# A fused top-k attention and gated feed-forward kernel: the start-up slots rearranged (whole-row scores, paired weight shifts, other chunk counts, two feed-forward items in slot 6)

## The chip, the cores and the metric

The kernel runs on one core of one Trainium2 chip. A core has five engines that work side by side, each through its own list of instructions in order: TensorE (PE, matrix products), VectorE (DVE), ScalarE (ACT), GpSimd (POOL) and SyncE (SP, which here only starts transfers). They wait for each other through semaphores. The metric is the time of one execution on the device in microseconds (us); three runs of the kernel before took 1415.8, 1416.53 and 1416.7 us, median 1416.53 us.

## The reference

Two blocks follow each other. The first is attention of 8 batches, 8 heads, 576 positions and 64 channels a head that keeps only the 32 largest scores of each row. The second multiplies every token by a first weight matrix, applies h·cos(h), and multiplies by a second one.

```python
scores = scale * np.matmul(q, k.transpose(0, 1, 3, 2))
kth = np.partition(scores, -top_k, axis=-1)[..., -top_k:-top_k + 1]
scores = np.where(scores >= kth, scores, -1000000000.0)
scores = scores - np.max(scores, axis=-1, keepdims=True)
attn = np.exp(scores)
attn = attn / (np.sum(attn, axis=-1, keepdims=True) + 1e-09)
attn_out = np.matmul(attn, v)                 # top_k = 32
x = attn_out.transpose(0, 2, 1, 3).reshape(4608, 512)
h = x @ w_in                                  # 512 x 2048
out = (h * np.cos(h)) @ w_out                 # 2048 x 512
```

All of it is computed to float32 accuracy; the two weight matrices arrive as 64-bit floats.

## The kernel before, in words

**Units and slots.** The 4608 tokens are cut into 36 blocks of 128 rows. A unit is one block of rows for one pair of heads, so there are 144 units, four to a block (`NP = 4`). The main loop calls `slot` once for each unit i from 0 to 143; the order in which `slot` issues instructions is the order on every engine. In slot i the DVE selects the top 32 of unit i, ACT and DVE finish the softmax of unit i-1 (`w`), and the probabilities of unit i-2 (`x`) are turned for the product with v. For the first slots they are turned by PE and ACT (`turn`), from slot 6 on by a copy on POOL (L411), a write to memory and a transposing transfer on SP's queue (`send`).

**The way of one unit.** `scores` makes the products of q and k on PE. A row of 576 scores does not fit one accumulator bank, so 448 columns go to a tile `sc` and the last 128 to a shared tile `rim`. Before the change the 128 rows of a unit are always computed as two halves of 64 rows (`halves_of`), since a block can straddle two batches; with two heads this is four products for `sc` and four for `rim`, each on a 64x64 quarter of the PE array. `take_scores` copies them to memory on ACT: L247 for the 448 columns, and L251 twice for the ends, once for each half of the rows, as the two halves put the heads into the banks in opposite order (`rim_bank`). Scores are computed one or two slots ahead, for two units in the even slots from slot 2 on.

The DVE then folds each row (columns j and j+288): L259 writes the larger of each two into `rest`, and POOL makes the smaller ones, `low`, by an integer sum (L275) and difference (L284). In slots 8 to 10 (`BUSY`) the DVE makes `low` itself (L267). `topk_round` runs four rounds of MAX8 (L351) and MATCH_REPLACE8 (L356) on `rest` and two on `low`. The first instruction of the next slot on the DVE is the reduction at L339, so the distance of two L339 is the length of a slot.

**Values and the feed-forward block.** In slots 5, 10, 14, 18 and so on, `values` multiplies the turned probabilities of the last four units by v (L473), and `take_values` scales the result into `xT` on the DVE (L489, L497). `take_values` stands in the last round of `topk_round`, before the last MAX8 pair on `low`. From `xT` the feed-forward block is fed in items: an `ff1` item is eight 128x128 products into half an accumulator bank (L551), an `ff2` item two products 128x512 (L626). The table `plan` says for each slot modulo 4 which kinds are tried at three places of the slot (`feed`); kind 0 is `ff1`, kind 1 is `ff2`. When a bank is full, `take_banks` copies it on ACT (L565, L567), then POOL reduces the argument (L587, L596), ACT takes the sine (L606, after loading its table, and L388 loads the table of the exponential again), and POOL multiplies (L613).

**Weights.** The two matrices come in 32 chunks of 128x512 (16 of `w_in`, 16 of `w_out`), loaded by `load_weights` (n chunks a slot) and decoded in three steps: ACT makes two float pieces (L133, L136, `decode_first`, near the end of a slot), the DVE shifts one of them left by three bits (L144, `decode_second`, one instruction a chunk, 128x512), and POOL adds the pieces (L154, `decode_third`). In slot 0 the last two steps stand at the end of the slot; in every later slot they stand between the third and the fourth round of the top-k. A `w_in` tile holds four chunks; `w_out` was 16 tiles.

Of the kernel before, what the change touches and what calls it, by code (L numbers as in the profile page):

```python
# [17 lines left out]
P = 128  # L18
# [12 lines left out]
def kernel(  # L31
# [52 lines left out]
    for i in range(DF // CW):  # L84
        w = consts.tile([P, NC, CW], F32, tag=f"w_in{i}", name=f"w_in{i}")
        w_in.append(w)
        for c in range(NC):
            cols = slice(words * i * CW, words * (i + 1) * CW)
            chunks.append((moe_w_in[c * P : (c + 1) * P, cols], w[:, c]))
    for f in range(NF):  # L90
        w = consts.tile([P, DM], F32, tag=f"w_out{f}", name=f"w_out{f}")
        w_out.append(w)
        chunks.append((moe_w_out[f * P : (f + 1) * P, :], w))
    CHUNKS, XB = 6, 3
# [8 lines left out]
    def load_weights(n, queue):  # L103
        for _ in range(n):
            i = wq["next"]
            if i >= len(chunks):
                return
            src, dst = chunks[i]
            if not DECODE:
                queue.dma_start(out=dst, in_=src)  # L110
                wq["next"] = wq["done"] = i + 1
                continue
            spare = i < 2 * NC + 10 and i % 2 == 1 and staged(1) < XB
            if spare:
                st = ffw.tile([P, CW, 2], I32, tag="x", name="st", bufs=XB)
            elif staged() + ff["live"] >= CHUNKS:
                return
            else:
                st = ffw.tile([P, CW, 2], I32, tag="g", name="st", bufs=CHUNKS)
            queue.dma_start(out=st.rearrange("p w i -> p (w i)"), in_=src)  # L120
            wq["loaded"].append((st, dst, int(spare)))
            wq["next"] = i + 1
# [4 lines left out]
    def decode_first(n):  # L127


        for _ in range(min(n, len(wq["loaded"]))):  # L130
            st, w, spare = wq["loaded"].popleft()
            lo, hi = st[:, :, 0], st[:, :, 1]
            nc.scalar.activation(  # L133
                out=w, in_=hi.bitcast(F32), func=AF.Prelu, scale=2.0**-111, alpha=2.0**32
            )
            nc.scalar.mul(out=lo, in_=lo.bitcast(U32), mul=2.0**-29)  # L136
            wq["second"].append((st, w, spare))

    def decode_second(n):

        for _ in range(min(n, len(wq["second"]))):
            st, w, spare = wq["second"].popleft()
            wi = w.bitcast(I32)
            nc.vector.tensor_scalar(  # L144
                out=wi, in0=wi, scalar1=3, scalar2=None, op0=ALU.logical_shift_left
            )
            wq["third"].append((st, w, spare))

    def decode_third():

        while wq["third"]:
            st, w, _ = wq["third"].pop()
            wi = w.bitcast(I32)
            nc.gpsimd.tensor_tensor(out=wi, in0=wi, in1=st[:, :, 0], op=ALU.add)  # L154
            wq["done"] += 1
# [6 lines left out]
    for t0 in range(0, B * S, P):  # L162
        parts, halves_of = [], []
        for i, a in enumerate((t0, t0 + TAIL)):
            b, q0 = a // S, a % S
            halves_of.append((b, q0, i * TAIL))
            if parts and parts[-1][0] == b:
                parts[-1][2] = P
            else:
                parts.append([b, q0, TAIL, i * TAIL])  # L170
        for hp in range(NP):
            units.append({"hp": hp, "tok": t0, "parts": parts, "halves_of": halves_of})
    NU = len(units)
# [56 lines left out]
    def scores(u):  # L230
        sc = u["sc"] = ps.tile([P, 2, 512], F32, tag="sc", name="sc", bufs=2)
        for to, k0, k1 in ((sc, 0, SB), (sc_ends[u["n"] % 2], SB, S)):
            for b, q0, r0 in u["halves_of"]:
                for j in range(2):
                    d = slice(j * D, (j + 1) * D)
                    st = pairs[b, u["hp"]]
                    nc.tensor.matmul(  # L237
                        to[r0 : r0 + TAIL, rim_bank(r0, j) if k0 else place(u["hp"], j), 0 : k1 - k0],
                        st["q"][d, q0 : q0 + TAIL],
                        st["k"][d, k0:k1],  # L240
# [4 lines left out]
    def take_scores(u):  # L245
        s = u["s"] = work.tile([P, 2, S], F32, tag="s", name="s", bufs=4)
        nc.scalar.copy(out=s[:, :, 0:SB], in_=u["sc"][:, :, 0:SB])  # L247
        ends = sc_ends[u["n"] % 2]
        for r0 in (0, TAIL):
            r, back = slice(r0, r0 + TAIL), rim_bank(r0, place(u["hp"], 0))  # L250
            nc.scalar.copy(out=s[r, :, SB:S], in_=ends[r, :: 1 - 2 * back])  # L251
# [64 lines left out]
    def topk_round(u, rnd, between=(), ahead=None):  # L316
# [11 lines left out]
        for k in range(TOPK // 16):  # L328
            more = k < TOPK // 16 - 1
            if ahead and not more:  # L330
                take_values(ahead)
            search(top[:, :, 1 + 8 * k : 9 + 8 * k, 1], low, low, more, () if more else between)
# [124 lines left out]
    def values(us):  # L457


        begun = set()  # L460
        for b, _, rows, r0 in us[0]["parts"]:
            r = slice(r0, r0 + rows)
# [188 lines left out]
    def can_second():  # L651
        if not second:
            return False
# [91 lines left out]
    def slot(i, u, w, x, z):  # L745
        n = (3, 4, 4, 4, 4, 3)[i] if i < NP + 2 else 2
        if i < NP:
# [10 lines left out]
        topk_round(u, 2)  # L758
        if i > 0:
            decode_second(NP)  # L760
# [4 lines left out]
        if z:  # L765
            take_banks()
        feed(*plan[i % NP][0])

# [15 lines left out]
        if i + 1 < NU:  # L784
            take_scores(units[i + 1])
        topk_round(u, 3, both(w), z)
        if i == 0:
# [103 lines left out]
```

## Time and profile before

The profiled execution took 1416.63 us; the profiler's span, from the first to the last instruction, is 1414.8 us, so 1.8 us lie outside it.

| | PE | DVE | ACT | POOL |
|---|---|---|---|---|
| busy us in the span | 1354.5 | 1346.2 | 1143.5 | 1164.6 |
| share of the span | 96% | 95% | 81% | 82% |

The DVE's slots, from the starts of its L339 instructions:

| slot | 1 | 2 | 3 | 4 | 5 | 6 | 7 | 8 | 9 | 10 | 11 | 12 | 13 |
|---|---|---|---|---|---|---|---|---|---|---|---|---|---|
| starts at us | 17.37 | 28.29 | 38.63 | 48.96 | 59.29 | 71.59 | 81.59 | 91.38 | 101.98 | 112.31 | 124.51 | 134.13 | 143.43 |
| length us | 10.92 | 10.33 | 10.34 | 10.33 | 12.30 | 10.00 | 9.79 | 10.59 | 10.33 | 12.20 | 9.62 | 9.29 | 8.99 |

From slot 13 on, three slots of four take 8.99 us and the fourth, which has the `xT` instructions, mostly 9.6 to 9.9 us. The last unit's slot starts at 1347.47 us; what follows is the rest of the feed-forward block.

How to read it: a busy share says how much of a stretch an engine had an instruction in work, not that it set the pace. The pace is seen where an engine stands idle and from what released it. PE's busy time is partly modelled and holds waiting that it cannot show; the granted clock of PE (the share of full speed) is printed beside it by stretches.

### The profile page before, as it was taken

The numbers are of one execution on the slowest core, as the hardware profiler recorded it, in microseconds if no ns is written. First come the engines' busy times: TensorE is split into PE (matmuls) and PEld (weight loads), VectorE is DVE, ScalarE is ACT, GpSimd is POOL, SyncE is SP. The second block draws the span as 40 slices with busy tenths as digits, with TensorE's granted clock in tenths as the row PEclk, the third lists the DMA queues.
The fourth block names the chain that finished last, engine by engine and source line by source line (L and its number), as shares of the span: only waits on it lengthen the run. The fifth ranks groups of instructions, "written<-read, shape, count | busy, mean of one in ns | idle before, by whom it ended". The sixth has DMA issues, their size and how long they took to land.

```text
span 1414.8 us, 32526 instructions
## 1 busy us (share of the span) xinstructions
PE 1354.5 (96%) x11328; PEld 975.1 (69%) x11328; DVE 1346.2 (95%) x5161; ACT 1143.5 (81%) x2050; POOL 1164.6 (82%) x804
## 2 busy tenths in 40 slices
PE   4567999999999999999999999999999999999998
PEld 2355777777777777777777777777777777777775
DVE  7999999999999999999999999999999999999931
ACT  7978888888888888888888888888888888888831
POOL 4778889888988888888888888888888898888810
PEclk6688999999999999999999999999999999999999
DMA  9575776566765566657665666656766566665540
GB/s 284 174 231 157 208 214 173 159 172 189 170 178 157 166 173 185 176 150 206 172 170 154 157 180 183 183 149 188 191 168 169 150 174 169 144 157 145 152 100 16
DMA packets 427445, 240.15 MB, mean 170 GB/s; under 512 B 375952, under 2 KB 392592, under 8 KB 427280
## 3 DMA queue, kind: packets, MB, share of 16 engines
q1 hardware_dynamic: 420720, 224.22, 58.2%
q10 hardware_dynamic: 6560, 13.85, 2.7%
q8 instruction: 89, 1.46, 0.4%
q14 instruction: 76, 0.62, 0.1%
HBM read 45.09 MB, written 101.19 MB: 103 GB/s over the span
## 4 chain that ended last, share of the span: by engine, by line
PE 82%; DVE 9%; ACT 6%; DMA 1%; POOL 1%; issue 0%; SPq 0%; ACTq 0%; DVEq 0%; POOLq 0%
PE o L626 32%; PE mm L551 32%; PE rim L473 10%; PE sc L237 7%; DVE top L351 4%; DVE rest L356 2%; PE rim L237 2%; DMA st<-in_moe_w_in_dram 1%; ACT s L388 1%; ACT s L380 1%; DVE rest L259 1%; ACT st L136 1%; DVE low L356 1%; ACT w_in L133 0%; ACT w_out L133 0%
## 5 line engine op out<-in xcount | busy, mean ns | idle before, releaser
L551 PEld LDWEIGHTS mm<-xT,w_in 128*128 128x128 f32 x4608 | 538.3, 192 | 78.7 <-issue 56.0
L551 PE MATMUL mm<-xT,w_in 128*128 128x128 f32 x4608 | 540.3, 276 | 10.1 <-ACT x L567 8.4
L626 PE MATMUL o<-w_out,g 128*128 128x512 f32 x1152 | 524.7, 599 | 0.0
L351 DVE MAX8 top<-rest 128x8 f32<-128x288 f32 x1152 | 479.0, 451 | 0.0
L356 DVE MATCH_REPLACE8 rest<-top,rest 128x288 f32<-128x288 f32 x864 | 376.7, 444 | 0.0
L626 PEld LDWEIGHTS o<-w_out,g 128*128 128x128 f32 x1152 | 207.7, 190 | 219.5 <-issue 219.2
L411 POOL COPY halves<-s 128x2304 uint16<-128x2304 uint16 x140 | 294.5, 2103 | 51.7 <-ACT s L388 48.4
L351 DVE MAX8 top<-low 128x8 f32<-128x288 f32 x576 | 241.9, 449 | 0.5 <-POOL low L284 0.5
L388 ACT ACTIVATE s<-s,nd 128x576 f32<-128x576 f32 x288 | 220.3, 768 | 0.8
L284 POOL TENSOR_TENSOR low<-low,rest 128x576 int32<-128x576 int32 x141 | 199.2, 1413 | 11.1
L380 ACT ACTIVATE s<-s,top 128x576 f32<-128x576 f32 x288 | 205.5, 761 | 0.0
L275 POOL TENSOR_TENSOR low<-s 128x576 int32<-128x576 int32 x141 | 198.8, 1410 | 6.6 <-ACT s L251 6.6
L378 ACT ACTIVATE nd<-nd 128x2 f32<-128x2 f32 x144 | 29.3, 204 | 175.4 <-DVE nd L371 175.4
L596 POOL TENSOR_TENSOR x<-g,x 128x1024 f32<-128x1024 f32 x68 | 160.8, 2365 | 5.7
L613 POOL TENSOR_TENSOR g<-g,x 128x1024 f32<-128x1024 f32 x68 | 160.8, 2364 | 0.0
L237 PE MATMUL sc<-k,q 64*64 64x448 f32 x1152 | 144.7, 570 | 12.3 <-DMA k<-in_k_dram 7.7
L473 PE MATMUL rim<-ring,v 128*64 128x128 f32 (+1 forms) x2560 | 138.3, 267 | 0.0
L473 PEld LDWEIGHTS rim<-ring,v 128*64 128x64 f32 x2560 | 129.2, 139 | 6.5 <-issue 6.0
L247 ACT COPY s<-sc 128x896 f32<-128x896 f32 x144 | 128.8, 894 | 3.3 <-PE sc L237 3.2
L251 ACT COPY s<-rim 64x256 f32<-64x256 f32 x288 | 105.9, 368 | 26.6 <-PE rim L473 24.9
L356 DVE MATCH_REPLACE8 low<-top,low 128x288 f32<-128x288 f32 x288 | 125.5, 444 | 0.0
L587 POOL TENSOR_SCALAR x<-x 128x1024 f32<-128x1024 int32 x68 | 71.1, 1046 | 63.0 <-ACT x L567 63.0
(55 smaller groups left out, 1269.7 us busy)
## 6 DMA issues: line engine op xcount, KB each, us to landing
rows<-halves SPq DMA_DIRECT2D x140, 640.0 KB, 3.2
out_dram<-ob ACTq DMA_DIRECT2D x36, 256.0 KB, 2.1
q<-in_q_dram SPq DMA_DIRECT2D x31, 288.0 KB, 3.4
st<-in_moe_w_in_dram SPq DMA_DIRECT2D x16, 512.0 KB, 7.0
v<-in_v_dram SPq DMA_DIRECT2D x32, 256.0 KB, 3.2
k<-in_k_dram SPq DMA_DIRECT2D x31, 144.0 KB, 3.4
k<-in_k_dram SPq DMA_DIRECT2D x32, 128.0 KB, 3.5
st<-in_moe_w_out_dram SPq DMA_DIRECT2D x8, 512.0 KB, 4.1
```

Of the source, the lines that this page charges most:

```text
L237: nc.tensor.matmul(to[r0 : r0 + TAIL, rim_bank(r0, j) if k0 else place(u["hp"], j), 0 : k1 - k0], st["q"][d, q0 : q0 + TAIL], st["k"][d, k ...
L275: nc.gpsimd.tensor_tensor(out=u["low"].bitcast(I32), in0=s[:, :, 0:HS], in1=s[:, :, HS:S], op=ALU.add)
L284: nc.gpsimd.tensor_tensor(out=low, in0=low, in1=u["rest"][:, :, HS:S].bitcast(I32), op=ALU.subtract)
L351: nc.vector.max(to[:, j], src[:, j])
L356: nc.vector.match_replace(rest[:, j], to[:, j], src[:, j], NEG)
L380: nc.scalar.activation(out=s[:, j], in_=s[:, j], func=AF.Prelu, bias=less[:, j, 1:2], scale=1.0, alpha=FAR)
L388: nc.scalar.activation(out=s[:, j], in_=s[:, j], func=AF.Exp, bias=nd[:, j : j + 1], scale=SCALE, accum_out=den[:, j, 0:1],)
L411: nc.gpsimd.tensor_copy(out=halves[:, :, 0 : 2 * S], in_=s.rearrange("p (k h) -> p h k", h=2))
L473: nc.tensor.matmul(to[d, r], lhsT, rhs, start=(bank, j) not in begun, stop=c == NT - 1 and u in us[-2:] and r0 + rows == P,)
L551: nc.tensor.matmul(mm[:, at : at + w], w_in[f // FC][:, c, (f % FC) * P : (f % FC + 1) * P], blk["xT"][:, c], start=c == 0, stop=c == NC - 1,)
L596: nc.gpsimd.tensor_tensor(out=x, in0=g, in1=x, op=ALU.subtract)
L626: nc.tensor.matmul(o, g[:, at : at + P], w_out[f], start=f == 0, stop=f == NF - 1)
```

## The change

It touches the first eleven slots; from slot 12 on both programs list the same instructions in the same order on every engine.

- **Scores.** For the units of the first 256 tokens (units 0 to 7) the rows are one part of 128, so `scores` issues two products for `sc` and two for `rim` instead of four and four, each 64 deep and 128 rows wide (half of the PE array, 64x128, instead of a quarter), and `take_scores` issues one end copy of 128x256 instead of two of 64x256.
- **Shifts.** `decode_second` takes two neighbouring chunks of the same tile with one instruction of 128x1024. `w_out` becomes one tile for that. 32 instructions become 19: 13 pairs and 6 single ones (pairs in slots 0 to 10: 1, 1, 2, 1, 1, 1, 2, 1, 1, 1, 1).
- **Place of the shifts in slot 1.** There the shift and POOL's addition move from before the fourth round to the place of `take_values`, before the last MAX8 pair on `low`.
- **Chunk counts.** The chunks decoded by ACT at the end of slots 0 to 9 were 3, 4, 4, 4, 3, 3, 2, 2, 2, 2 and are 3, 4, 3, 4, 3, 4, 2, 2, 2, 2 (three more come before slot 0 in both). One chunk thereby moves from slot 2 to slot 5 on ACT and SP, and from slot 3 to slot 6 on DVE and POOL.
- **First product.** Slot 6 feeds two `ff1` items instead of one at its first place, slot 9 two instead of three, so that banks fill one slot earlier: the first sines come in slots 8 and 10 instead of 9 and 11. `can_second` gets a bound so that no `ff2` item comes before slot 10, as it was.

```diff
+    w = consts.tile([P, NF, DM], F32, tag="w_out", name="w_out")
     for f in range(NF):
-        w = consts.tile([P, DM], F32, tag=f"w_out{f}", name=f"w_out{f}")
-        w_out.append(w)
-        chunks.append((moe_w_out[f * P : (f + 1) * P, :], w))
+        w_out.append(w[:, f])
+        chunks.append((moe_w_out[f * P : (f + 1) * P, :], (w, f)))
...
-        for _ in range(min(n, len(wq["second"]))):
-            st, w, spare = wq["second"].popleft()
-            wi = w.bitcast(I32)
+        left = min(n, len(wq["second"]))
+        while left:
+            st, (w, c), spare = wq["second"].popleft()
+            wq["third"].append((st, (w, c), spare))
+            m = 1
+            if left > 1 and wq["second"][0][1][0] is w:
+                wq["third"].append(wq["second"].popleft())
+                m = 2
+            left -= m
+            wi = w[:, c : c + m].bitcast(I32)
             nc.vector.tensor_scalar(
                 out=wi, in0=wi, scalar1=3, scalar2=None, op0=ALU.logical_shift_left
             )
-            wq["third"].append((st, w, spare))
...
-            if parts and parts[-1][0] == b:
+            if t0 < 2 * P and parts:
                 parts[-1][2] = P
...
-            for b, q0, r0 in u["halves_of"]:
+            for b, q0, rows, r0 in u["parts"]:
...
-                        to[r0 : r0 + TAIL, rim_bank(r0, j) if k0 else place(u["hp"], j), 0 : k1 - k0],
-                        st["q"][d, q0 : q0 + TAIL],
+                        to[r0 : r0 + rows, rim_bank(r0, j) if k0 else place(u["hp"], j), 0 : k1 - k0],
+                        st["q"][d, q0 : q0 + rows],
...
-        for r0 in (0, TAIL):
-            r, back = slice(r0, r0 + TAIL), rim_bank(r0, place(u["hp"], 0))
+        for _, _, rows, r0 in u["parts"]:
+            r, back = slice(r0, r0 + rows), rim_bank(r0, place(u["hp"], 0))
...
-        if not second:
+        if not second or ff["now"] < 2 * NP + 3:
             return False
...
-        n = (3, 4, 4, 4, 4, 3)[i] if i < NP + 2 else 2
+        n = (3, 4, 3, 4, 3, 4)[i] if i < NP + 2 else 2
...
-        if i > 0:
+        if i > 1:
             decode_second(NP)
             decode_third()
...
-        feed(*plan[i % NP][0])
+        feed(*((0, 0) if i == NP + 2 else plan[i % NP][0]))
...
-        topk_round(u, 3, both(w), z)
+        def ahead():
+            if z:
+                take_values(z)
+            if i == 1:
+                decode_second(NP)
+                decode_third()
+
+        topk_round(u, 3, both(w), ahead)
```

`ff["now"]` is the slot's number plus one. `ahead` is called where `take_values` was, between the last replacement and the last MAX8 pair.

## The prediction

> **What bounds the kernel now.** I read the stretches first, then what the DVE waited for, then the order of time around each wait.
>
> ```profile
> 20.00:40.00 20.00, 10.01 (x58) 5.46 (x58) 20.00 (x73) 19.17 (x39) 15.08 (x13) 0.58 0.95 296
> 60.00:80.00 20.00, 15.88 (x173) 14.15 (x174) 18.39 (x70) 16.71 (x35) 14.48 (x13) 0.83 0.51 154
> 900.00:1200.00 300.00, 300.00 (x2469) 216.54 (x2468) 299.88 (x1160) 252.86 (x452) 263.98 (x179) 1.00 0.63 170
> ...
> DVE rest L259 <- ACT s L251: 7.7, 3, 6.8
> DVE xT L489 <- ACT s L251: 1.6, 1, 1.6
> DVE top L351 <- POOL low L284: 0.5, 1, 0.5
> DVE xT L497 <- ACT s L251: 0.3, 1, 0.3
> DVE rest L259 <- ACT st L136: 0.2, 1, 0.2
> ```
>
> The columns of the stretches are PE, PEld, DVE, ACT, POOL, then the clock. From 900 to 1200 us the DVE rests 0.12 us in 300. PE reads 300.00, but its time is partly modelled; the slots of 8.99 us are the DVE's own instructions end to end, so the DVE sets the pace. As both programs are the same from slot 12 on, what the DVE has gained at slot 13 is kept to the end. The second part (total, times, longest, us) is the whole of the DVE's waiting before 145 us but 0.8 at launch. This is where each wait and each touched instruction lies:
>
> ```profile
> 7.05 0.74 ACT L251 COPY s<-rim 64x256 f32<-64x256 f32 x2
> 7.83 0.76 DVE L259 TENSOR_TENSOR rest<-sc,s 128x576 f32<-128x576 f32 x1 [6.82 <-ACT s L251]
> 16.38 1.08 DVE L144 TENSOR_SCALAR w_in<-w_in 128x512 int32<-128x512 int32 x3
> 22.82 1.40 POOL L284 TENSOR_TENSOR low<-low,rest 128x576 int32<-128x576 int32 x1
> 23.15 2.03 DVE L144 TENSOR_SCALAR w_in<-w_in 128x512 int32<-128x512 int32 x3
> 34.08 1.43 DVE L144 TENSOR_SCALAR w_in<-w_in 128x512 int32<-128x512 int32 x4
> 62.01 0.39 ACT L438 COPY ring<-rim 128x256 f32<-128x256 f32 x1
> 63.52 5.73 PE L473 MATMUL rim<-ring,v 128*64 128x128 f32 x64
> 69.30 0.74 ACT L251 COPY s<-rim 64x256 f32<-64x256 f32 x2 [3.17 <-PE rim L473]
> 70.08 0.69 DVE L489 TENSOR_TENSOR xT<-rim,ring 128x512 f32<-128x512 f32 x1 [1.61 <-ACT s L251]
> 78.60 3.80 POOL L154 TENSOR_TENSOR w_out<-w_out,st 128x512 int32<-128x512 int32 x3 [3.27 <-ACT s L251]
> 86.23 1.41 POOL L284 TENSOR_TENSOR low<-low,rest 128x576 int32<-128x576 int32 x1
> 87.37 0.89 DVE L144 TENSOR_SCALAR w_out<-w_out 128x512 int32<-128x512 int32 x2
> 105.01 1.15 ACT L606 ACTIVATE x<-x,halfpi 128x1024 f32<-128x1024 f32 x1 [1.42 <-POOL x L596]
> 113.18 0.76 DVE L259 TENSOR_TENSOR rest<-sc,s 128x576 f32<-128x576 f32 x1 [0.65 <-ACT s L251]
> ```
>
> See that three shifts take 1.08 us alone, but 2.03 while POOL is inside L284; that the xT of slot 5 starts when an ACT copy ends, and that copy when PE's values end; and that a sine (105.01, slot 9) waits for POOL and is followed by a late score copy (113.18, slot 10).
>
> **The first unit, -0.35 us.** The first L259 starts when the second end copy ends. One copy of 128x256 from the same tile takes 0.39 (L438) where the two take 0.74: 0.35 less. Its products come before. Eight instructions on quarters took 1.99 us there; four on halves are not in this trace. Side by side in twos they do the same work in the same time: 0. One after the other they would at most double, +2.0; fewer weight loads could give back up to the 0.55 us they took. The nearest row is L473: once at full clock (at 155.77) its 64 take 3.71, 0.058 each, where L551's on the whole array take 0.117 (540.3 over 4608), so halves by columns do run together; halves by rows I take to do the same: 0. For the later units PE idles before its scores and ACT has them 2 us before the DVE asks.
>
> **Pairs, -0.8 us.** From three (1.08) to four (1.43) one more shift costs 0.35, while one alone lasts 0.42. A fixed part saved by a pair lies between 0 and the 0.14 that the xT rows give (512 columns 0.69, 256 columns 0.415, so 0.138 at none). Some 0.08 of that overlaps the next instruction: 0.06. Thirteen pairs, all on the pacing engine: 0.8 (0 to 1.8).
>
> **Slot 1, -0.5 us.** The first shift, asked at 23.15, got through only as L284 ended at 24.22: 0.95 lost. Placed later, the MAX8 pair comes first (0.73) and the pair on `low` waits from 23.88 to 24.25 for the same L284: 0.4. POOL idles from there until its additions, so the shifts run free. Nothing on POOL waits for them but L154.
>
> **Slot 5, -1.5 us.** ACT runs without a gap from 20.7 to 66, so the values start when ACT gets to L438 (62.0), not when its input is there (PE's product after the reciprocal, 59.8). The change takes out of ACT's row four end copies of 0.37 (slots 1 to 4) and one chunk of 1.13: 2.6. L438 then ends near 59.5, the values (6.8 us) near 66.3, the single copy 0.4 later at 66.8. The DVE asked at 68.47; by now it is 1.6 earlier (0.35 + 0.5 + seven pairs 0.4 + 0.35 for the shift that slot 3 gave to slot 6) and asks at 66.85. The wait of 1.61 falls to 0.1 or less. On SP's queue one chunk's issue (0.5 us) moves from slot 2 to slot 5; the next there is the write of POOL's halves after 72 us, so nothing waits. The cover is the clock: the 64 take 3.71 at full clock, here 5.73 at 0.83; at the 0.58 of the row 20 to 40 they would take some 7, and 1 us of the wait is back.
>
> **Slots 6 to 9, +1.65 us.** Here the stall that went comes back. The extra chunk of slot 5 costs ACT 1.13 and the two copies L565 and L567 come into slot 6 (1.2): ACT waited 2.9 us in slot 7 and covers both. PE's second item takes 2 us before the scores of unit 7, which ACT fetches 3 us later: nothing. POOL has no such cover. In slot 6 it adds four chunks, not three (1.26 each), while DVE time of slot 6 grows 0.2. Counted from the slot's start: L154 at 7.2, the copy L411 at 12.25, L275 at 14.65, L284 at 16.1 (14.64 before), its end at 17.5. The DVE asks for slot 7's shift at 16.0 (15.78 before, when it lost 0.14 to L284). If it gets in between L275 and L284, L284 ends 0.6 later and the MAX8 on `low` waits 0.8; if L284 is first, the shift waits 1.5. I take the first: +0.65 net, with 1.4 as the bound. Behind it POOL does two additions, L587 and L596, now in slot 7, and the sine of slot 8 waits for L596: at 3.5 us after slot 8 begins, where slot 9's came at 3.0. From the sine to the end of the end copy ACT needs 8.14 (105.01 to 113.15), so unit 9's scores come 11.65 into slot 8, and the DVE asks at 10.45 (slot 8 without its idle, and 0.14 of the next): a wait of 1.2, with all of slot 9 behind it. Slot 8's own idle 0.2 has no row that explains it; I count it gone.
>
> By a rule of the Trainium skill (SBUF — State Buffer, Who interferes with whom) VectorE's two-port instructions and GpSimd hold the shared port pair as an exclusive lock for the whole instruction, first come first served. It agrees with 2.03 against 1.08, and speaks against longer shifts: a pair locks POOL out for 0.6 at a time. By it the order at slot 7, 0.1 us apart in my count, decides 0.8 or 1.5.
>
> **Slots 10 to 12, -1.4 us.** Slot 9 has no sine now, so the 0.65 at 113.18 goes. Slot 10 has it, but its xT waits for PE's values anyway (0.35, stays; 0.45 at worst). In slot 11 POOL has L613 (2.37) where it had L587 and L596 (3.4) ahead of L275, so the 0.53 for `low` goes; and ACT, without a sine, ends the wait of 0.2 at slot 12.
>
> **Sum.** -0.35 -0.8 -0.5 -1.5 +1.65 -1.4 = -2.9 us (the shift moved from slot 3 to 6 cancels). Against the span 1414.8 that is 1411.9; with the 1.8 outside it 1413.7 for the profiled execution, which lies 0.1 above the median. So 1413.6 us. A measurement of this kernel can tell about 0.2%, 2.8 us, from no change: the line is 1413.7.
>
> **Rivals.**
> - *POOL's chain has room.* If POOL is quicker by some 0.8 us in slots 6 and 7, slot 7 loses nothing (0.65 + 0.14 less) and unit 9 waits 0.8 (the sine's cost in its own slot), not 1.2: 1412.4. For it: the count is off by 0.1 at one place. Against: L284 already met the shift before, with one addition less.
> - *The covers fail.* The shift waits out L284 (+0.7, of which unit 9's wait gives 0.6 back), and the values run at the low clock (+1.0), or pairs save nothing (+0.8): 1414.7 to 1415.5, no change to be told.
> - *Slower: a worse phase at every xT.* From 145 to 1340 us the DVE waited for the copy before xT only four times, 2.0 us in all, 0.6 at the longest. If the new start left PE behind the DVE, each of some 33 blocks could pay up to that 0.6: +20 -2.9, 1433.5. It decides from 0.09 a block, and reaches +0.2% at 0.17. Against: slots 12 on are the same program, and PE restarts in slot 10 from the same DVE instruction (L267), so both shift together.
> - *Slower too: the pair leaves the quick rate.* At the 1.08 ns a column of the xT rows a pair would take 1.17, not 0.6: 13 times 0.57 is +7.4, 1421. Against: the operands are the same, only longer; the change does less than it says from 0.7 a pair on.
>
> **How the numbers follow.** Forecast 0.52, a little more than half of it below 1413.7, since its own value lies there. POOL has room 0.27. Covers fail 0.14. Phase 0.04, slow pair 0.03. Faster 0.31 + 0.27, and 0.01 of the third case where only the clock's part comes: 0.59; slower 0.04 + 0.03 = 0.07; same 0.34. The forecast's own range is 1412.8 to 1414.4 (pairs 0 or 1.4; slot 7 at its bound). For the whole, 1411.6 is the POOL case less 0.8 for pairs at their upper bound, 1415.2 takes in most of the third case; the slower ones and its rest stay out.
>
> **What would show it.** L259 first at 7.5; the shifts of slot 1 in about 0.95 us after the replacement on `low`; xT of slot 5 with under 0.3 of idle; in slot 7 an L144 of over 1 us or a wait of MAX8 for L284; unit 9's L259 waiting for ACT about 1 us, unit 10's not; slot 13 starting near 140.6. Wrong if slot 13 starts after 142.5 or before 139, or if later slots are not 8.99.

## The result, and the profile after

The changed kernel takes 1419.7 us (median of 20 runs, 1416.0 to 1421.4), the kernel before 1416.0 in the same comparison (20 runs, 1414.9 to 1418.9): the ratio is 1.0022, 95% interval 1.0016 to 1.0028. So it is slower by some 3 us, where 1413.6 was forecast. The profiled execution took 1420.27 us with a span of 1418.3, against 1416.63 and 1414.8.

The lead of the DVE, that is how much earlier its slots begin than before, tells where that comes from (the terms are the prediction's, added up to that slot; the shift that moved from slot 3 to slot 6 counts 0.35 on its way):

| the DVE's lead at the start of slot | 2 | 6 | 10 | 13 | 14 | 15 | 144 |
|---|---|---|---|---|---|---|---|
| by the terms of the sum, us | 1.0 | 3.1 | 1.4 | 2.9 | 2.9 | 2.9 | 2.9 |
| measured, us | 0.87 | 3.23 | 0.86 | 1.76 | 1.76 | -2.65 | -3.57 |

The lead also holds the launch, which varies from one execution to the next: in the twelve profiled runs with whole-row scores the first fold starts between 6.55 and 7.66 us, in the four with halves between 7.44 and 7.86. So a lead is good to about 1 us, while the lengths of most slots repeat to a few hundredths.

Up to slot 14 the change won 1.76 of the 2.9 us counted. Then one slot, which both programs list alike, took 14.06 us instead of 9.65. The DVE's waits of the changed kernel from 5 to 170 us (what waits, for whom, us in total, times, longest) show it as the longest new one (4.3, at `xT` L497); the 1.5 before `den`, in slot 6, is new as well:

```profile
DVE rest L264 <- ACT s L256: 7.5, 3, 6.6
DVE xT L497 <- ACT s L256: 4.3, 1, 4.3
DVE den L401 <- ACT s L393: 1.5, 1, 1.5
DVE xT L505 <- ACT s L256: 1.2, 1, 1.2
DVE top L356 <- POOL low L289: 0.3, 1, 0.3
```

The stretches of the changed kernel (start and end, length, then PE, PEld, DVE, ACT, POOL, the clock, DMA share, GB/s):

```profile
20.00:40.00 20.00, 9.75 (x42) 5.87 (x42) 19.71 (x74) 19.05 (x41) 15.78 (x13) 0.59 0.93 295
60.00:80.00 20.00, 17.62 (x173) 15.85 (x169) 18.50 (x66) 13.07 (x26) 16.07 (x13) 0.89 0.51 149
155.00:160.00 5.00, 3.18 (x30) 2.85 (x32) 3.82 (x14) 2.45 (x6) 4.22 (x3) 0.66 0.47 166
900.00:1200.00 300.00, 299.68 (x2470) 216.75 (x2469) 299.11 (x1159) 251.19 (x447) 263.90 (x181) 1.00 0.64 171
```

From 900 to 1200 us the DVE still sets the pace, with 0.89 us of rest instead of 0.12. New is the row of slot 14: PE is without work for 1.8 us of five, and its clock falls to 0.66 there.

The timeline of the changed kernel in slots 0 to 6 (start, us, engine, line; in brackets the idle time and what ended it):

```profile
7.63 0.76 DVE L264 TENSOR_TENSOR rest<-sc,s 128x576 f32<-128x576 f32 x1 [6.61 <-ACT s L256]
23.98 0.82 DVE L356 MAX8 top<-low 128x8 f32<-128x288 f32 x2 [0.29 <-POOL low L289]
66.85 0.68 DVE L497 TENSOR_TENSOR xT<-rim,ring 128x512 f32<-128x512 f32 x1
74.15 1.28 DVE L151 TENSOR_SCALAR w_out<-w_out 128x1024 int32<-128x1024 int32 x2
75.57 5.05 POOL L160 TENSOR_TENSOR w_out<-w_out,st 128x512 int32<-128x512 int32 x4 [1.74 <-issue]
76.89 0.60 ACT L573 ACTIVATE g<-mm 128x512 f32<-128x512 f32 x1 [4.61 <-POOL w_out L160]
79.60 0.16 DVE L401 TENSOR_REDUCE den<-dens 128x2 f32<-128x4 f32 x1 [1.50 <-ACT s L393]
```

The fold comes earlier, slot 1 loses 0.29 to `low`, and slot 5's `xT` (66.85) has no wait before it. The last three rows are a surprise in slot 6: ACT's bank copy L573 stands 4.61 us until POOL has finished its first addition, because its target `g` takes a buffer of the staging tiles that POOL's additions set free; the exponentials (L393) queue behind it, and the DVE waits 1.50 for their sums.

The timeline of the changed kernel around slot 14, SP's queue, PE and the DVE:

```profile
140.44 2.78 SPq L453 DMA_TRANSPOSE ring<-rows  x1
143.27 0.57 SPq L199 DMA_DIRECT2D q<-in_q_dram  x1
...
145.74 0.53 SPq L447 DMA_DIRECT2D rows<-halves  x1
149.68 2.86 SPq L453 DMA_TRANSPOSE ring<-rows  x1
156.82 0.69 PE L481 MATMUL rim<-ring,v_tail 64*64 64x128 f32 x4 [2.55 <-DMA ring<-rows]
157.44 4.86 PE L481 MATMUL rim<-ring,v 128*64 128x128 f32 x64
163.14 0.76 DVE L497 TENSOR_TENSOR xT<-rim,ring 128x256 f32<-128x256 f32 x2 [4.31 <-ACT s L256]
```

The same places in the kernel before:

```profile
139.86 2.80 SPq L448 DMA_TRANSPOSE ring<-rows  x1
142.72 0.57 SPq L194 DMA_DIRECT2D q<-in_q_dram  x1
...
145.19 0.53 SPq L442 DMA_DIRECT2D rows<-halves  x1
149.50 2.76 SPq L448 DMA_TRANSPOSE ring<-rows  x1
155.23 0.62 PE L473 MATMUL rim<-ring,v_tail 64*64 64x128 f32 x16
155.77 3.71 PE L473 MATMUL rim<-ring,v 128*64 128x128 f32 x64
```

Read upwards: the `xT` waits for an ACT copy, ACT for PE's values, PE 2.55 us for the transposing transfer of unit 11; after that standstill the 64 products take 4.86 us, not the 3.71 that they take in slot 14 of the kernel before. There the `xT` (160.49) waits for nothing. SP's rows have not come earlier with the DVE: the transfer of slot 13 starts at 149.68 us where it started at 149.50, although slot 14 begins 1.76 us sooner. The transfers of the changed kernel from 149.4 to 157.2 us (queue 8 carries instructions; the last number of an issue is us to landing):

```profile
q8 instruction: 1, 0.02, 0.8%
...
out_dram<-ob ACTq DMA_DIRECT2D x1, 256.0 KB, 4.0
...
ring<-rows SPq DMA_TRANSPOSE x1, 7.1
```

In the kernel before the same transfer takes 4.9 us and has landed 2.0 us after slot 14 begins; here it lands 6.1 after, though the DVE itself is 1.76 us earlier. In its window lie the first write of the output and one packet of instructions, 16 KB, in work from 154.62 to 155.67 us. The write is issued 0.7 us into slot 14 in both kernels, and in the kernel before the transfer had 1.3 us left by then. The packet came there at 148.87, before the transfer began.

### The profile page after: what moved, and what is told of

Read it like the earlier page. It is cut to its first block, busy times and chain, and to the rows that moved or that the text cites. A ratio compares the mean times of both kernels' runs of the same rounds, so it can differ in the third digit from the quotient of the medians.

```text
span 1418.3 us, 32365 instructions
## 1 busy us (share of the span) xinstructions
PE 1358.5 (96%) x11264; PEld 979.5 (69%) x11264; DVE 1344.4 (95%) x5148; ACT 1140.3 (80%) x2042; POOL 1165.0 (82%) x804
## 4 chain that ended last, share of the span: by engine, by line
PE 83%; DVE 14%; ACT 1%; DMA 1%; issue 0%; POOL 0%; SPq 0%; DVEq 0%; ACTq 0%; POOLq 0%
PE o L634 32%; PE mm L559 32%; PE rim L481 10%; PE sc L242 7%; DVE top L356 6%; DVE rest L361 4%; PE rim L242 2%; DVE rest L264 1%; DVE low L361 1%; DMA ring<-rows 1%; DVE w_in L151 0%; ACT s L393 0%; DMA st<-in_moe_w_in_dram 0%; PE warm L849 0%; ACT s L385 0%
## 5 line engine op out<-in xcount | busy, mean ns | idle before, releaser
L393 ACT ACTIVATE s<-s,nd 128x576 f32<-128x576 f32 x288 | 220.3, 768 | 0.8
L289 POOL TENSOR_TENSOR low<-low,rest 128x576 int32<-128x576 int32 x141 | 199.2, 1413 | 11.1
L242 PE MATMUL sc<-k,q 64*64 64x448 f32 (+1 forms) x1120 | 147.5, 568 | 16.4 <-DVE low L272 10.6
L256 ACT COPY s<-rim 64x256 f32<-64x256 f32 (+1 forms) x280 | 103.1, 368 | 29.8 <-PE rim L481 28.3
L595 POOL TENSOR_SCALAR x<-x 128x1024 f32<-128x1024 int32 x68 | 71.1, 1046 | 64.6 <-ACT x L575 64.6
```

What stands on the lines that cost most here:

```text
L242: nc.tensor.matmul(to[r0 : r0 + rows, rim_bank(r0, j) if k0 else place(u["hp"], j), 0 : k1 - k0], st["q"][d, q0 : q0 + rows], st["k"][d, k ...
L289: nc.gpsimd.tensor_tensor(out=low, in0=low, in1=u["rest"][:, :, HS:S].bitcast(I32), op=ALU.subtract)
L393: nc.scalar.activation(out=s[:, j], in_=s[:, j], func=AF.Exp, bias=nd[:, j : j + 1], scale=SCALE, accum_out=den[:, j, 0:1],)
```

## The experiments

Three theories of the 4.31 us: *the output write* lies in the transfer's way; *SP's queue*, which works in order, sends the write of POOL's halves late, behind the loads of q and k (halves ready at 143.28, loads 143.27 to 145.65, write 145.74); *the instruction list*: half the score products of eight units are gone, in the profile 64 products and as many weight loads, 128 instructions, so that PE fetches the next 16 KB of its list at other moments. All runs are compared with runs of the kernel before on the same chip at the same time (its medians beside the experiments were 1415.6, 1416.4, 1417.2 and 1418.0 in the four groups, so the ratios count, not the times). "Landed" is unit 11's transfer and "fetches" the 16 KB packets, both in us from the start of slot 14.

| kernel | us | ratio, 95% interval | slot 6 | slot 14 | landed | xT wait | fetches |
|---|---|---|---|---|---|---|---|
| before | | | 10.00 | 9.65 | 2.0 | 0 | -3.6, 5.5 |
| after | 1419.7 | 1.0022 [1.0016, 1.0028] | 11.80 | 14.06 | 6.1 | 4.31 | -14.0, 4.0 |
| e1_out_other_queue | 1418.19 | 1.0019 [1.0009, 1.0028] | 11.8 | 11.99 | 5.5 | 2.25 | -13.8, 3.3 |
| e2_late_unit_last | 1415.74 | 1.0000 [0.9991, 1.0009] | 11.8 | 11.87 | 8.0 | 2.13 | -13.4, 5.7 |
| e3_one_item_slot6 | 1414.21 | 0.9985 [0.9974, 0.9996] | 10.20 | 10.00 | 5.8 | 0.25 | -14.8, 3.6 |
| e4_banks_after_scores | 1414.45 | 0.9994 [0.9985, 1.0004] | 10.20 | 10.18 | 3.1 | 0.44 | -14.8, 3.1 |
| e5_pe_count_restored | 1416.82 | 0.9994 [0.9983, 1.0005] | 11.80 | 12.60 | 6.1 | 2.85 | -23.9, -4.7 |
| e6_only_first_product_undone | 1417.52 | 1.0005 [0.9995, 1.0016] | 10.20 | 14.17 | 6.0 | 4.43 | -14.7, 3.8 |
| e8_scores_alone | 1419.09 | 1.0014 [1.0005, 1.0024] | 10.00 | 15.09 | 6.8 | 5.22 | -13.7, 4.7 |
| e10_loads_on_act_queue | 1414.84 | 0.9990 [0.9981, 1.0000] | 11.80 | 10.12 | 3.6 | 0.37 | -13.6, 3.9 |
| e11_one_item_and_act_queue | 1413.53 | 0.9973 [0.9962, 0.9984] | 10.20 | 9.66 | 2.5 | 0 | -15.1, 3.2 |
| e14_and_late_unit_last | 1413.88 | 0.9974 [0.9964, 0.9984] | 10.20 | 10.00 | 3.1 | 0.26 | -15.1, 3.3 |
| e12_before_loads_on_act_queue | 1416.11 | 0.9988 [0.9974, 1.0001] | 9.99 | 11.15 | 4.6 | 1.40 | -2.7, 7.4 |
| e13_pairs_and_slot1_alone | 1415.69 | 0.9995 [0.9985, 1.0004] | 9.93 | 9.65 | 1.7 | 0 | -4.3, 5.6 |
| e15_before_list_longer | 1425.18 | 1.0056 [1.0035, 1.0077] | 10.00 | 14.46 | 6.3 | 4.72 | -14.8, 4.3 |
| e16_scores_alone_list_restored | 1414.16 | 0.9977 [0.9963, 0.9990] | 10.00 | 9.65 | 1.9 | 0 | -4.1, 6.1 |

### The transfer's neighbours

**e1_out_other_queue**: the changed kernel, block 0's output write on SP's queue, behind the transfer.

```diff
-        nc.scalar.dma_start(out=out[row : row + P, :], in_=ob)
+        (nc.sync if row == 0 else nc.scalar).dma_start(out=out[row : row + P, :], in_=ob)
```

> The changed kernel, with the first block's output write (rows 0 to 127) issued from SP's queue behind the loads of v instead of from ACT's queue. Theory (the write collides with unit 11's transposing transfer in slot 13): that transfer falls from 7.1 us to 5 to 6, the wait of xT in slot 14 from 4.3 to under 2.5 us, the time from 1419.7 to about 1417.5 or less. Rival (the transfer is held up by an instruction fetch of 16 KB, or the queue is late anyway): it stays at about 7 and the wait at about 4, time 1419.7.

The transfer takes 6.37 us instead of 7.10, PE waits 1.90 instead of 2.55: by this the output write is a part of the matter, the smaller one. The wait of `xT` falls by more, 2.06 us, because the 64 products behind take 3.71 us again; the granted clock from 155 to 160 us is 1.00 in this run. The time (1.0019) is not told apart from the changed kernel's (1.0022).

**e2_late_unit_last**: in slot 14 the products of unit 11 come last of the four units'.

```diff
-            for c in (NT, *range(NT)):
-                for u in us:
+            late = us[-1:] if us[0]["tok"] == 2 * P and len(us) == NP else []
+            for c, some in [(c, [u for u in us if u not in late]) for c in (NT, *range(NT))] + [
+                (c, late) for c in (NT, *range(NT))
+            ]:
+                for u in some:
```

> The changed kernel, with the products of unit 11 put last among the values of slot 14 (60 of 80 instructions come before them), nothing else. Theory (all of the loss is PE standing before unit 11's rows and then running at a lower clock): the wait of xT in slot 14 falls from 4.3 us to under 0.5, slot 13's gain of 1.8 us is kept to the end: 1415.97 - 1.8 = about 1414.2, and the runs no longer spread over 5 us. Rival (the loss only moves to another wait of the next slots): over 1417.

PE can work longer before it needs the transfer, but this time that landed 8.0 us after the slot's start, and half the wait is left. The gain, 0.2% on the changed kernel, shows that the stall hangs on PE's need of unit 11; why that is late it doesn't tell.

### Slot 6

**e3_one_item_slot6**: e2 with one item fed in slot 6, as before the change.

```diff
-        feed(*((0, 0) if i == NP + 2 else plan[i % NP][0]))
+        feed(*plan[i % NP][0])
```

> As the run with unit 11 last, and slot 6 feeds one first-product item again. Theory (ACT's bank copy in slot 6 stood 4.6 us before a buffer that POOL's addition of slot 6 frees, and held the exponentials behind it): the DVE's waits of 1.5 and 0.3 us in slots 6 and 7 go; slot 7's shift then meets POOL (0.8 to 1.5 us back), and slot 10 has its wait of about 0.65 again; slot 7 starts near 78.6, the time 1413.5 to 1414.5. Rival (the wait comes from PE's late products): slot 7 starts at 80.2 still.

**e4_banks_after_scores**: e2 with two items, but slot 6's bank copies on ACT stand behind its copy of the scores.

```diff
-        if i % NP != 3:
+        if i % NP != 3 and i != NP + 2:
             take_banks()
...
-        take_banks()
+        if i != NP + 2:
+            take_banks()
         if i + 1 < NU:
             take_scores(units[i + 1])
+        take_banks()
```

> As the run with unit 11 last, and in slot 6 ACT takes the full bank only after the exponentials and the score copy. Theory: the wait for the buffer is hidden behind them, slot 7 starts near 78.6 instead of 80.2; slot 7's shift meets POOL (0.8 us back, or 1.5); time 1413 to 1414. Rival: ACT meets the same wait later and unit 8's scores come late, slot 8 gives it all back: 1414.2 as with unit 11 last alone.

Both bring slot 6 from 11.80 to 10.20. In e4 the bank is still copied in slot 6, only later: so it is the order on ACT, with the exponentials behind a copy that waits for a buffer, and not the second item's work. Not all of the 1.6 us stays: counted from the start of slot 6 to that of slot 14, e3 is 0.8 us shorter than e2 and e4 0.4, as the waits come back in slots 11 and 12 (e3: 10.06 and 9.30 us instead of 8.98 and 8.99) or in slots 8 and 10 (e4). In the times, the intervals of e2, e3 and e4 overlap. Now that the DVE is not late, slot 7 shows what the prediction had counted for it (timeline of e3, DVE and POOL):

```profile
83.42 0.69 DVE L151 TENSOR_SCALAR w_out<-w_out 128x1024 int32<-128x1024 int32 x1
83.50 1.88 POOL L289 TENSOR_TENSOR low<-low,rest 128x576 int32<-128x576 int32 x1
85.41 0.82 DVE L356 MAX8 top<-low 128x8 f32<-128x288 f32 x2 [0.57 <-POOL low L289]
```

The pair gets in 0.08 us ahead, L289 takes 1.88 instead of 1.41, and MAX8 waits 0.57 for it; 0.8 had been expected.

**e6_only_first_product_undone**: that edit of e3 on the changed kernel, with nothing else.

> The changed kernel with one part undone: slot 6 feeds one item of the first product as before the change, and no order of slot 14 is touched. Theory A (the two items of slot 6 cost about 1.6 us in slots 6 and 7, and slot 14 is a matter of SP's queue and the phase of the transfers): slot 6 takes 10.2, no wait of 1.5 there; the sine is back in slots 9 and 11; slot 14 keeps a wait between 0.3 and 4.3, as the transfers fall: 1414.5 to 1418.5. Rival B (the two items are the cause of the stall in slot 14 as well, through the earlier first product and the earlier second one): slot 14 takes under 10.2 and the time is 1413.5 to 1414.5. If the transfer of unit 11 still takes over 6 us and the wait is over 3, the two items have no part in it.

Slot 6 is mended, and slot 14 is as bad as ever (wait 4.43, transfer 7.01). The two items cost 1.6 us in slot 6, of which 1.2 are left at slot 14 (slots 11 and 12 grow again, to 9.99 and 9.29), and they have no part in the stall of slot 14. It also shows that e3's calm slot 14 came from e2's order.

### Which part of the change makes the transfer late

**e8_scores_alone**: the kernel before with the scores' part alone. Its `halves_of` gets a row count and one entry for units 0 to 7, otherwise two.

```diff
-            halves_of.append((b, q0, i * TAIL))
+            if not whole:
+                halves_of.append((b, q0, TAIL, i * TAIL))
+            elif i == 0:
+                halves_of.append((b, q0, P, 0))
...
-        for r0 in (0, TAIL):
+        for _, _, rows, r0 in u["halves_of"]:
```

> The kernel before with the scores' part alone: whole rows for units 0 to 7 and one end copy each; shifts, chunk counts and the first product as before. Theory A (terms of the sum): the first fold 0.2 to 0.35 us earlier, slot 5's xT wait falls from 1.6 by the four end copies of 0.37 that ACT no longer has, less the 0.35 that the DVE gained: to about 0.4 to 0.6; slots 1 to 4, 6 and 7 unchanged; the sum -1.4, time 1414.5 if slot 14 keeps its 9.65. Rival B (the shorter list of PE moves its fetches onto the transfers of slots 10 to 14): the transposing transfer of slot 13 takes over 6 us, slot 14 takes 11 us or more, time 1416 to 1418.

Rival B, and by more than it said: slot 14 takes 15.09 us. The start and slot 5 gain 1.9 us together (slot 5's wait goes entirely), 2.2 with slot 8 and what follows, and the one stall takes back more than twice that.

**e13_pairs_and_slot1_alone**: the kernel before with the pairs and the place of slot 1's shifts; PE's list keeps its length.

> The kernel before with the shifts alone: two chunks a time, one tile for w_out, and in slot 1 the shifts behind the last replacement; scores, chunk counts and first product as before, and PE's list is as long as before. By the terms of the sum: pairs -0.8, slot 1 -0.5, slot 5's wait grows by what the DVE has gained until then (about 0.7, since ACT's row is not shorter), so that some -0.6 to -0.9 is left at slot 10, which its xT wait takes up in part: 1415.3 to 1416 beside 1416. If the instruction fetches keep their place relative to the transfers (PE's list is unchanged), the transfer of slot 13 takes under 5.5 us and slot 14 under 10. Rival (any gain before slot 13 meets the late transfer, whatever PE's list): the transfer over 6 us, slot 14 over 11, 1417 or more.

Slot 14 takes 9.65 us, as before. Slots 1 to 4 win 1.0 us (0.60 in slot 1, then 0.11 to 0.14 a slot), but slot 5's `xT` wait grows from 1.61 to 3.20, as ACT's row, not the DVE, sets it there; that is more than the 0.7 expected. So this part alone keeps nothing, and it does not stall. With a lead of 0.06 us at slot 14 it can't tell whether an early DVE would stall by itself; e16 does.

**e5_pe_count_restored**: the changed kernel with 32 tiny products on PE, early, where it idles.

```diff
+    def fill(u):
+        n = 0 if u["n"] == 0 else 8 if u["n"] == 7 else 4
+        for _ in range(n):
+            nc.tensor.matmul(u["sc"][0:TAIL, 0, SB : SB + 8], ident[:, 0:TAIL], ident[:, 0:8], start=True, stop=True)
...
             scores(m)
+            if m["n"] < 2 * NP:
+                fill(m)
```

> The changed kernel with 32 products of 64x8 added on PE (four after the scores of units 1 to 6, eight after unit 7; nothing uses their results), so that PE's list is as long again as before the change, 64 instructions more (a product and a weight load each). Theory A (instruction fetches: shorter by 64 instructions, PE fetches its 16 KB pieces of the list at other moments, and one falls on unit 11's transfers): the write of slot 10 lands within 3.3 us of its issue (5.08 in the changed kernel, 2.93 before), the transposing transfer of slot 13 within 5.3 us (7.10 and 4.90), the xT wait of slot 14 is under 1 us, time 1415.0 to 1416.5. Rival B (the transfer is late because SP's queue is behind and the output write of block 0 lies in its way; the fetch is a bystander): transfer 6.5 to 7.5 us, xT wait 3.5 to 4.5, time 1419 to 1420. Between them: the fetch moves but the transfer gains only the 1 us that it held, wait 3, 1418.5.

Between the theories. The profile counts each listed product twice, 64 products and 64 weight loads more, 128 instructions and not the 64 of the expectation, so the list is indeed as long as before. The time is not told apart from that of the kernel before, slot 10's write takes 2.93 us, as theory A had it, and the transfer 5.44, just over its 5.3. But a fetch now lies in slot 13's write (at 145.03, in work for 2.29 us; the write takes 6.37 us, and the loads of k beside it take 5.5 to 5.9), so the transfer starts late instead of running long, and a wait of 2.85 is left: a miss of theory A's time.

**e16_scores_alone_list_restored**: e8 with the same 32 products.

> The kernel before with the scores' part alone (1419.09 us), and 32 products of 64x8 added on PE (four after the scores of units 1 to 6, eight after unit 7; nothing uses their results), so that PE's list has its old length. Theory A (the length of the list made that part slower): transfer of slot 13 under 5.6 us, slot 14 under 11, time 1414.5 to 1416. Rival B (whole-row products or the earlier DVE made it slower): transfer over 6.5, slot 14 over 13, 1418 or more.

Theory A. The DVE's waits from 5 to 170 us, of e8 and then of e16:

```profile
DVE rest L263 <- ACT s L255: 7.5, 3, 6.7
DVE xT L493 <- ACT s L255: 5.2, 1, 5.2
DVE top L355 <- POOL low L288: 0.8, 1, 0.8
```

```profile
DVE rest L269 <- ACT s L261: 7.3, 3, 6.5
DVE top L361 <- POOL low L294: 0.5, 1, 0.5
DVE xT L507 <- ACT s L261: 0.4, 1, 0.4
```

The 5.2 is gone. The same scores, the same gains up to slot 14, and work added to PE: 0.9977 instead of 1.0014. What made the scores' part slower was that it made PE's list shorter.

The transfers of the two runs show the way. In e8 the fetch at -13.7 lies in the write of slot 12's halves, which takes 5.72 us; in e16 it takes 3.36, with no fetch in it. So slot 12's transfer starts at 140.14 us instead of 137.78, and behind it on SP's queue come the loads, the write of slot 13 and unit 11's transfer, which starts 0.6 us before slot 14 instead of 3.2. Then the fetch at 4.7 lies in that transfer, and it takes 7.39 us instead of 5.02. Each fetch goes with about half of the 5 us by which the landing differs. The changed kernel has the same pattern: fetches in the writes of slots 10 and 12 (5.08 and 4.30 us; 2.93 and 3.39 in the kernel before) and in unit 11's transfer.

**e15_before_list_longer**: the kernel before, with nothing changed but 96 such products (13 after the scores of units 1 to 6, 18 after unit 7): in the profile 192 products and 192 weight loads, 384 instructions (the expectation counts half). That is 128 short of two packets of 256, which puts the fetches where a list 128 shorter has them, as the changed kernel's is.

> The kernel before with 96 products of 64x8 added on PE (13 after the scores of units 1 to 6, 18 after unit 7; nothing uses their results): 192 instructions more, which is 64 short of the 256 that a fetch of 16 KB would hold at 64 bytes each, so that the fetches fall at the same products as in the changed kernel; the DVE's list and all transfers are as before. Theory A (the place of the fetch decides): a 16 KB fetch between 3 and 5.5 us after slot 14 begins (2.2 us before it in the kernel before... 148.87 against 152.42), the transposing transfer of slot 13 takes 6.3 to 7.4 us instead of 4.90, and the xT wait of slot 14 is 1 us or more; time 1417 to 1419. Rival B (the changed kernel's DVE, 1.8 us early, is needed, as SP's queue then is not ready): the transfer may be slow but lands before PE asks; slot 14 stays under 10 and the time within 0.8 us of the kernel before.

The transfers from 154.3 to 161.6 us of e15:

```profile
q8 instruction: 1, 0.02, 0.8%
...
out_dram<-ob ACTq DMA_DIRECT2D x1, 256.0 KB, 4.1
...
ring<-rows SPq DMA_TRANSPOSE x1, 7.2
```

The fetch comes 4.3 us after slot 14 begins, the transfer takes 7.16 us and slot 14 14.46, with a wait of 4.72; slot 12's write, with the fetch at -14.8 in it, takes 5.28 us instead of 3.39. A packet of another engine's list (queue 14, 0.43 us) comes at the same moment; e8 has none in its transfer, which took 7.39. No early DVE is needed, as slot 14 begins 2.9 us later here than in the kernel before: rival B falls. The time is worse than theory A's 1419: slot 5 also grew, from 12.30 to 15.50 us, where its `xT` waited 3.57 us and a fold 1.15; I take that for the added products' own cost there, which was not tested. There are only four runs of this kernel.

### SP's queue

**e10_loads_on_act_queue**: the changed kernel, loads of q, k and v in slots 10 to 13 issued by ACT (`load_qk` and `load_v` take the queue as an argument).

```diff
-            load(b, hp)
+            load(b, hp, nc.scalar if i < 14 else nc.sync)
```

> The changed kernel with the loads of q, k and v in slots 10 to 13 issued from ACT's queue and not from SP's, so that on SP the write of POOL's halves is not behind them. Theory A (SP's queue, in order, makes the transfers late): in slot 13 the write goes out within 0.5 us of POOL's halves (2.5 in the changed kernel), the transposing transfer of unit 11 is issued 1.5 to 2.4 us earlier (147.3 to 148.2, not 149.7), PE's wait for it falls from 2.55 to under 0.6 and the xT wait of slot 14 from 4.31 to under 1.5; time 1416 to 1417. Rival B (the transfer is slow because of what else the DMA engines carry): issued earlier, it takes longer, lands after 155.5 and the wait stays over 3; 1419. [...]

Theory A, though the time fell below its range. SP sends slot 13's write at 143.81 instead of 145.74; the transfer starts at 147.03, still takes 6.74 us, and PE no longer waits for it. `xT` waits 0.37, and the changed kernel gains 0.3%.

**e12_before_loads_on_act_queue**: the same on the kernel before.

> The kernel before with nothing changed but the queue of the q, k and v loads in slots 10 to 13 (ACT's in place of SP's). There the transfer of unit 11 lands at 154.40, before PE asks, and the xT of slot 14 waits for nothing: by the theory that SP's queue decides only where the DVE comes early, the time stays, within 0.8 us of the kernel before. Rival (the queue was a cost in the kernel before as well): 1 us or more faster, slot 14 under 9.3.

Not told apart from no change by its interval, which leaves room for a gain of 0.26%. In the profiled execution slot 14 is even worse (11.15; the transfer of slot 12 took 9.44 us with the loads now beside it). So a gain of the queue by itself is not shown; in the changed kernel it gave room where fetches had taken it.

**e11_one_item_and_act_queue**: e10 with e3's one line, so both costs undone.

> The changed kernel with the two costly things undone together: slot 6 feeds one item, and the loads of q, k and v in slots 10 to 13 go out on ACT's queue. If the two costs are separate (1.6 us in slot 6 and 4 us in slot 14, by the runs with one of them undone), slot 6 takes 10.2, slot 14 begins near 148.9 and takes about 10, slot 15 begins near 159, and the time is 1412.5 to 1413.5: faster than both kernels. Rival (the transfers only move onto other work as the DVE comes earlier): slot 14 takes 11.5 or more, 1415 to 1416.

The two costs are separate, and this is a version faster than both kernels: 0.9973. With no load between them on SP, the write of slot 13 goes at 142.61 and its transfer at 146.38 us; that takes 6.08 us and still lands 2.5 us into slot 14.

**e14_and_late_unit_last**: e11 with e2's order.

> As the run before (one item in slot 6, loads on ACT's queue), and in slot 14 the products of unit 11 with v come last of the four units, so that PE has 48 products of work before it needs unit 11's transfer. If the transfer of unit 11 still lands late in some executions, this takes 0.3 to 1 us off and narrows the spread of the times: 1412 to 1413. If the queue alone was the matter, no difference to the run before (within 0.5 us).

No difference to e11. With the transfer there in time, the order of the products is worth nothing; the spread is the same 1.6 to 1.9 us.

## Why the prediction was wrong

**The step that failed** is the sentence "As both programs are the same from slot 12 on, what the DVE has gained at slot 13 is kept to the end." The lists are the same; the place of PE's instructions in its list is not. Nothing in the prediction asked how unit 11's probabilities reach PE: through a write, a transposing transfer and SP's queue, which in the kernel before were done 2.0 us into slot 14, while PE came to unit 11's first product some 3.2 us into it (an estimate: three quarters into the 0.62 us at 155.23). With fetches at about -14 and +4 us the landing moved to 6.1, the 1.2 us of room were gone, and the DVE lost 4.41 us in a slot that was to cost it nothing. That the length of PE's list is the cause is shown from both sides: e15 makes the stall in the kernel before by lengthening that list, and e16, with the list's old length, has the gains of e8 (2.3 us at slot 14) without the stall.

**The rival on the slow side** ("a worse phase at every xT") had the right place, an `xT` behind PE's values, with the wrong mechanism: one block pays 4.31, not 33 blocks 0.6 each. It was put aside by the same sentence as the forecast.

**Start (-0.35), slot 1 (-0.5), slot 5 (-1.5), pairs (-0.8)**: right as mechanisms. The single copy takes 0.38 instead of 0.74, and the first fold is 0.20 earlier, which the spread of the launch does not let one execution show; its four products on halves took 2.27 us where eight on quarters took 1.99, which had been put at 0. Slot 1 lost 0.29 to `low` instead of 0.4. Slot 5's wait is gone, the lead at slot 6 is 3.23 against 3.1. The pairs were a little underrated: two take 1.20 us from the start of the first to what follows, 0.60 each where two single ones step 0.70, so 0.10 saved, not 0.06.

**Slots 6 to 9 (+1.65)**: too low, and with wrong parts. With the moved shift and five pairs the terms take 1.7 us off the lead; it fell by 2.37. Missing was the wait of slot 6, 1.50 and 0.28: the sum let "ACT waited 2.9 us in slot 7" cover the bank copies and did not ask when their target buffer comes free. Since the DVE was late by that, the meeting with L284 in slot 7 did not happen here; e3 and e6 show it, at 0.57 and 0.58. Unit 9's wait was 0.65, not 1.2; slot 8's idle time went, as counted.

A rule of the Trainium skill (SBUF — State Buffer, Who interferes with whom) was set beside that step: the shared port pair is held for a whole instruction, first come first served. e3's rows agree in the order: the pair that came 0.08 us ahead made L289 0.47 us longer, where 0.61 us of the pair were left.

**Slots 10 to 12 (-1.4)**: 0.9 was won. The waits in slots 10 to 12 for the score copy and for `low` went, but slot 10's `xT` waited 1.19 instead of 0.35 (0.45 had been the bound): the 64 products there took 4.99 us instead of 4.21. They began 1.6 us earlier, in stretches that grant PE a clock of 0.50 (112 to 117 us) and 0.81 (117 to 122), the same in both kernels.

**After slot 15** another 0.9 us is lost over 129 slots, of which 0.8 is one `xT` wait at 1046 us behind one more late transfer (PE waits 0.32 there).

**Open**: the trace doesn't say on which DMA engine a packet runs, so that the fetch delays the transfer is shown by moving it and by where it lies, not by a queue seen waiting. The times of the changed kernel spread over 5 us, four of 20 below 1417; that those executions had no stall was not seen, as one execution is profiled. And e5's wait shows that the old length of the list is no cure: what counts is where the fetch falls.

## What to carry to other kernels

Before "the rest is the same program" is used, follow each input of the first stage behind the change back to its transfer, and note how long before its use it lands: here 1.2 us of room decided over 4 us. A change in the number of PE's instructions moved its instruction fetches against the transfers; where a result depends on such a phase, try the change again with a few idle instructions added before judging it. A copy whose target comes out of a shared pool waits for that pool's last reader, and holds everything behind it on its engine.

## What the runs showed of the hardware

**Instruction fetches lie among the other transfers.** In the kernel before, 22,656 instructions of PE (11,328 products and as many weight loads) go with 89 packets of 16 KB on the instruction queue, in the changed kernel 22,528 with 88: 255 and 256 instructions a packet. One is in work for 1.07 us in the mean in the kernel before, 1.13 in the changed one. Between 112 and 1340 us of the changed kernel, a transposing transfer with such a packet wholly inside it takes 6.18 us (median of 35), any other 4.85 (98); a write of the halves 4.57 (19) and 3.12 (114). A longer transfer is likelier to hold a packet, but of the 98 others none took over 5.9 us, while 21 of the 35 took over 6; in the kernel before, none of 104 others and 13 of 29. PE has room for nearly all of them: between 112 and 1340 us it waited for such a transfer twice, 2.9 us in all. The Trainium skill has the size (Advanced Engine Details and Errata, ISA Cache: a line of 16 KB holds 256 instructions), which agrees with the counts.

**A short standstill can lower PE's clock, and its length alone does not decide.** After waits of 2.55 us (the changed kernel), 2.58 (e6), 2.90 (e15) and 3.43 (e8) the granted clock of the 5 us behind (155 to 160 us, in e15 160 to 165) was 0.66, 0.66, 0.74 and 0.72, and the 64 products that follow took 4.86, 5.38, 5.38 and 5.10 us instead of 3.71. After 2.75 us (e5) and 1.90 (e1) it stayed at 1.00, and they took 3.71. So a stall of PE of 2.55 us cost the DVE 4.31 where the clock fell, and one of 2.75 cost it 2.85 where it did not.
